# Attention with a relative bias and a bilinear feed-forward: where the third batch's Q and K are transposed, and how the first loads are cut and queued

## The chip, the cores and the metric

The kernel runs on one core of a Trainium2 chip. The metric is the device time of one execution in microseconds (us), as the median of several runs. A profile is taken of one execution; its span runs from the first to the last instruction of the program.

## What is computed

The reference, cut to what matters:

```python
batch, n_heads, seq, head_dim = (8, 8, 576, 64)
scores = scale * np.matmul(q, k.transpose(0, 1, 3, 2))       # scale = 1/8
bucket = np.where(is_small, n, large)                         # n = |i - j|, 32 buckets
scores = scores + bias_table[bucket].transpose(2, 0, 1)[None, :, :, :]
attn = np.exp(scores - np.max(scores, axis=-1, keepdims=True))
attn = attn / (np.sum(attn, axis=-1, keepdims=True) + 1e-09)
x = np.matmul(attn, v)             # to (4608, 512): tokens x (head, dim)
out = (x @ w_a) * (x @ w_b) @ w_out                          # d_ff = 1536
```

All inputs and the output are float32 in HBM; the kernel computes in bfloat16 with float32 sums.

## The kernel before

**Tiling.** Two heads of a batch make a pair: 32 pairs, four to a batch, numbered `p`; pair `p` belongs to batch `p // 4`. The 576 positions of a head are four blocks of 128 ("main") and a tail of 64; the tails of a pair's two heads share one 128-row tile (`ktl`, `qtl`, `vt`) with zeros in the other half. For each pair `qk1` (L330) makes the scores of one block of keys for both heads into one PSUM tile, `ex` (L343) takes the exponential on ScalarE, `mul` (L349) multiplies by the exponential of the bias on VectorE with a reversed window of `W`, `qk_tail`, `ex_tail` and `mul_tail` do the tails, `av` (L385) multiplies by v with a column of ones for the row sum, `norm` (L437) divides, and `t_x` (L452) transposes the result into `xn`. The bias tables `W` and `Wt` come from a small matmul of `bias_table` with a one-hot constant (`oh`, L171 and L216), an exponential (L219), a store to HBM (`bias_tab`) and overlapping reads of it (`load_w`, L165).

**Q and K turned.** The scores need Q and K with the head dimension on partitions. Pairs 0 to 3 are transposed by TensorE in float32 at the start (`q_next`, `k_next`, `tails_next`, L568 to L586). For later batches `early(b)` (L118) decides: where it is true, `t_q` and `t_k` (L282, L302) transpose on TensorE in bfloat16, four blocks each and for `t_k` also the two tail tiles (`t_tails`, L296), and `c_q`, `c_k` copy to `QT` and `KT` on VectorE; where it is false, `turn` (L318) has SyncE's queue transpose a whole batch by DMA into `QTb`, `KTb`, `QTt`, `KTt`. Before, batches 0 and 1 are early; batch 2 is turned by DMA in steps 6 and 7 (`turns`, L692).

**The feed-forward part.** Nine chunks of 512 tokens, each 24 units `ff_a`/`ff_b` (four matmuls into one PSUM bank, read by ScalarE into `ha` or by VectorE into `g_sb`, L505 and L511) and 12 units of `ff_o` (four matmuls each, three units to an output tile, L515). `w_a` and `w_b` lie in `NW` parts of `WC` columns, loaded by `load_w_in` (L156).

**The order of the work** is written out by hand; each engine executes its instructions in the order in which they are recorded. Pairs 0 to 2 run in a loop (L588), pair 3 and the first scores of pair 4 in a listed sequence (L636 to L684), and steps 4 to 32 in a loop (L701) in which step `s` does the scores of pair `s` and the products of pair `s - 1`. A step has markers `U`; at each marker `put_units` emits feed-forward units until the step's quota (6, 7, 7, 7, 6 for steps 4 to 8, then 9) is spread over the step. Unit 24, the first that needs `wo`, falls in step 7.

**Buffers.** PSUM has two tiles for scores, and banks `AV` (one), `TR` (one) and `FF` (two). From step 8 (`ring3`, L707) the feed-forward units use `FF` and `TR` in turn, three banks; then the tail scores of a pair and `av` of blocks 3 and 4 go to `AV` instead of `TR` (L364, L704).

**The loads.** q, k, v and the weights change type while they are loaded, and go by GpSimd's queue, in program order: the tables and v of batch 0, pair 4's q, k and batch 1's tails, two parts of the weights, the rest of batch 1 with the third part between, three parts of weights, batch 2's q and k, `wo`, clears of the second tail tiles, batch 2's tails, and then the later batches. A queue's loads use eight semaphores in turn, so each load issued waits for the one eight before it. The float32 q and k of batch 0 come by SyncE's and ScalarE's queues, the DMA transposes and the output stores by SyncE's.

Of the kernel before, what the change touches and what calls it, by code (L numbers as in the profile page):

```python
# [13 lines left out]
def kernel(  # L14
# [11 lines left out]
    nc = tc.nc  # L26
    FP32 = mybir.dt.float32
    BF16 = mybir.dt.bfloat16
# [78 lines left out]
    KT = [wpool.tile([128, SM + 256], BF16, name=f"KT{i}") for i in range(2)]  # L107
    XG = [wpool.tile([128, 5, 2, Dh], BF16, name=f"XG{i}") for i in range(4)]

    NW = 6  # L110
    WC = DF // NW
    wa_sb = [wpool.tile([128, NMC, WC], BF16, name=f"wa{i}") for i in range(NW)]
    wb_sb = [wpool.tile([128, NMC, WC], BF16, name=f"wb{i}") for i in range(NW)]
# [2 lines left out]
    g_sb = [wpool.tile([128, DM], BF16, name=f"g{df}") for df in range(NDF)]  # L116

    def early(b):  # L118
        return b < 2

    def load_t(src, dst, b, h0, h1):
        for t in range(NM):
            nc.gpsimd.dma_start(  # L123
                out=(vm[b % 2][:, h0:h1, t, 0:Dh] if dst is None else
                     dst[b % 2][:, :].rearrange("p (t h d) -> p t h d", h=H, t=NM)[:, t, h0:h1, :]),
                in_=src[b, h0:h1, 128 * t:128 * t + 128, :].transpose([1, 0, 2]))
# [7 lines left out]
    def load_p(src, dst, b, hp):  # L134
        x = dst[b % 2][:, :].rearrange("p (t h d) -> p t h d", h=H, t=NM)
        for h in (2 * hp, 2 * hp + 1):
            load_h(nc.gpsimd, src, x[:, :, h, :], b, h)

    def load_vp(b, hp):
        for h in (2 * hp, 2 * hp + 1):  # L140
            load_h(nc.gpsimd, v, vm[b % 2][:, h, :, 0:Dh], b, h)

    def load_pad(eng, src, dst, b, nb):
        for hh in range(2):
            eng.dma_start(
                out=dst[64 * hh:64 * hh + 64, 4 * (b % 2):4 * (b % 2) + 4 * nb, hh, 0:Dh],
                in_=src[b:b + nb, hh:H:2, SM:S, :].rearrange("b h c d -> c (b h) d"))

    def load_tails(b, nb):
        load_pad(nc.gpsimd, k, ktl[b // 2 % 2], b, nb)  # L150
        load_pad(nc.gpsimd, q, qtl[b // 2 % 2], b, nb)
# [4 lines left out]
    def load_w_in(part):  # L156
        for src, dst in ((moe_w_a, wa_sb), (moe_w_b, wb_sb)):
            nc.gpsimd.dma_start(
                out=dst[part][:, :, :],
                in_=src[:, WC * part:WC * part + WC].rearrange("(m p) n -> p m n", p=128))  # L160
# [4 lines left out]
    def load_w(eng, hp):  # L165
        eng.dma_start(out=W_sb[hp][:, :, :],
                      in_=bass.AP(tensor=tab, offset=2 * hp * TB, ap=[[1, 128], [TB, 2], [1, 384]]))

    nc.sync.dma_start(out=bt_sb[0:NB, :], in_=bias_table)
    nc.scalar.dma_start(out=cst[:, :], in_=cst_handle.ap())  # L170
    nc.gpsimd.dma_start(out=oh_sb[0:NB, :], in_=oh_handle.ap())  # L171
    def pad(eng, x, n):
        eng.memset(x[0:64, :, 1, 0:n], 0.0)
        eng.memset(x[64:128, :, 0, 0:n], 0.0)
# [17 lines left out]
    pad(nc.vector, qt32, Dh)  # L192
    pad(nc.vector, kt32, Dh)
    load_pad(nc.sync, q, qt32, 0, 1)
    nc.vector.tensor_copy(out=id32[:, :], in_=ident)
    for i in range(2):
        nc.vector.memset(vm[i][:, :, :, Dh:Dh + 1], 1.0)
# [11 lines left out]
    def warm_up(n):  # L209
        for _ in range(n):  # L210
            nc.tensor.matmul(out=warm[:, :], lhsT=zero_sb[:, 0:128], rhs=zero_sb[:, :],
                             start=True, stop=True)

    warm_up(4)
    tps = ps_av.tile([128, 512], FP32, tag="av", name="tab_ps")
    nc.tensor.matmul(out=tps[0:H, 0:NR], lhsT=bt_sb[0:NB, :], rhs=oh_sb[0:NB, :],  # L216
                     start=True, stop=True)
    warm_up(5)
    nc.scalar.activation(out=tab_sb[0:H, 127:127 + NR], in_=tps[0:H, 0:NR], func=ACTF.Exp)  # L219
    nc.scalar.dma_start(out=tab.ap(), in_=tab_sb[0:H, :])  # L220
    load_pad(nc.scalar, k, kt32, 0, 1)

    load_w(nc.gpsimd, 0)
    for hh in range(2):
# [3 lines left out]
    load_vp(0, 0)  # L228
    load_vt(0, 1)
    load_w(nc.gpsimd, 1)  # L230
    load_vp(0, 1)
    load_w(nc.gpsimd, 2)
    load_t(v, None, 0, 4, 8)
    load_w(nc.gpsimd, 3)
    load_p(q, qn, 1, 0)
    load_p(k, kn, 1, 0)
    load_tails(1, 1)
    load_w_in(0)
    load_w_in(1)
    load_vp(1, 0)  # L240
    load_vt(1, 1)
    load_t(q, qn, 1, 2, 8)
    load_t(k, kn, 1, 2, 8)
    load_w_in(2)
    load_t(v, None, 1, 2, 8)

    st = [dict() for _ in range(NP + 1)]
# [27 lines left out]
    def bank(where, dt, name):  # L275
        return where[0].tile([128, 512 if dt is FP32 else 1024], dt, tag=where[1], name=name)
# [5 lines left out]
    def t_q(p, where):  # L282
        if p >= NP or not early(p // 4):
            return
        ps = bank(where, BF16, f"trq{p}")
        for t in range(NM):
            nc.tensor.transpose(ps[:, 128 * t:128 * t + 128], blocks(qn, p)[:, t, :, :], ident)
        st[p]["q"] = ps
# [13 lines left out]
    def t_k(p, where):  # L302
        if p >= NP or not early(p // 4):
            return
        ps = bank(where, BF16, f"trk{p}")
        for t in range(NM):
            nc.tensor.transpose(ps[:, 128 * t:128 * t + 128], blocks(kn, p)[:, t, :, :], ident)
        if p > 3:
            t_tails(p, ps, SM)
        st[p]["k"] = ps  # L310

    def c_k(p, eng=None):
        if p >= NP or not early(p // 4):
            return
        n = SM + 256 if p > 3 else SM
        copy(eng, KT[p % 2][:, 0:n], st[p]["k"][:, 0:n])

    def turn(b, what):  # L318
# [38 lines left out]
    def qk_tail(p):  # L357
        ps = ps_sc.tile([128, 2, 512], FP32, tag="sc", name=f"qkt{p}")
        for t in range(NM):
            nc.tensor.matmul(  # L360
                out=ps[:, 0, :].rearrange("p (h t c) -> p h t c", h=2, t=NM)[:, :, t, :],
                lhsT=kT_(p, t), rhs=qTt_(p), start=True, stop=True)
        nc.tensor.matmul(out=ps[:, 1, :], lhsT=kTt_(p), rhs=qT_(p), start=True, stop=True)  # L363
        pt = bank(TR if p < 8 else AV, FP32, f"qktt{p}")  # L364
        for hh in range(2):
            nc.tensor.matmul(out=pt[:, 0:ST], lhsT=kTt_(p), rhs=qTt_(p)[:, ST * hh:ST * hh + ST],
                             start=(hh == 0), stop=(hh == 1))
        st[p]["ps"] = (ps, pt)
# [252 lines left out]
            t_x(s - 1)  # L621
        qk1(s + 1, 1)

    load_w_in(3)
    load_w_in(4)
    load_w_in(5)
    load_t(q, qn, 2, 0, 8)
    load_t(k, kn, 2, 0, 8)
    load_w_out()
# [6 lines left out]
    ex(3, 0)  # L636
    mul(2, 3)
    mul_tail(2)
    t_q(4, TR)
    c_q(4)  # L640
    t_k(4, FF)
    av(2, 0)
    av(2, 1)
    qk1(3, 2)
    ex(3, 1)
    av(2, 2)
    norm(2, 0)
    c_k(4)
    qk_tail(3)
    ex(3, 2)  # L650
    av(2, 3, FF)
# [6 lines left out]
    t_x(2, FF)  # L658
    mul(3, 1)
    av_part(3, 0)  # L660
    qk1(4, 0)
    av_part(3, 1)
    mul(3, 2)
    av_part(3, 2)
    mul_tail(3)
    ex(4, 0)
    av_part(3, None)
    c_x(2)
    mul(3, 3)
    qk1(4, 1)  # L670
    av_part(3, 3)
# [9 lines left out]
    c_x(3)  # L681
    qk1(4, 3)
    ex(4, 3)
    qk_tail(4)  # L684

    def load_qkt(b):
        load_t(q, qn, b, 0, 8)
# [3 lines left out]

    def turns(s):  # L692
        b = s // 4 + 1
        if b == 2:
            for x in {6: "qk", 7: "t"}.get(s, ""):
                turn(b, x)
        elif 2 < b < B and s % 4 < 3:
            turn(b, "qkt"[s % 4])

    quotas = {4: 6, 5: 7, 6: 7, 7: 7, 8: 6}  # L700
    for s in range(4, NP + 1):  # L701
        new = s < NP
        U = "unit"
        A = lambda *jq: (lambda: [av(s - 1, j, AV if j < 3 or s > 7 else TR) for j in jq])  # L704
        N = lambda j: (lambda: norm(s - 1, j))
        steps = []
        if s == 8:  # L707
            ring3 = True
        if s == 4:
            steps += [U, lambda: ex_tail(4), lambda: mul(4, 0), U, lambda: mul(4, 1), U, lambda: mul(4, 2),  # L710
                      U, lambda: mul(4, 3), lambda: mul_tail(4), U, lambda: t_q(5, TR), lambda: c_q(5),
                      U, lambda: t_k(5, TR), lambda: c_k(5)]
        elif new:
            e = early((s + 1) // 4)
            steps += [lambda: qk(s, 0), lambda: ex(s, 0), U, lambda: ex(s, 1), A(0, 1, 2), N(0), U,
                      lambda: mul(s, 0), A(3, 4), N(3)]
            if s - 1 in XD:
                steps += [lambda: t_x(s - 1), lambda: turns(s)]
            steps += [U, lambda: mul(s, 1), lambda: qk(s, 2), lambda: ex(s, 2)]
            if e:  # L720
                steps += [lambda: t_q(s + 1, TR), lambda: c_q(s + 1)]
            steps += [U, lambda: ex(s, 3)]
            if e:
                steps += [lambda: t_k(s + 1, TR), lambda: c_k(s + 1)]
            steps += [U, lambda: mul(s, 2), U, lambda: mul(s, 3),
                      lambda: qk_tail(s), lambda: ex_tail(s), U]
            if s - 1 not in XD:
                steps += [lambda: t_x(s - 1, TR), lambda: c_x(s - 1), lambda: turns(s)]
            steps += [U, lambda: mul_tail(s), U]
        else:  # L730
            steps += [A(0, 1, 2), N(0), U, A(3, 4), N(3), U, lambda: t_x(s - 1, AV),
                      lambda: c_x(s - 1), U, U, U, U, U, U, U]
        quota = quotas.get(s, 9)
        seen, put = 0, 0
        nu = sum(1 for x in steps if x is U)
        for x in steps:
            if x is U:
                seen += 1
                n = (quota * seen + nu - 1) // nu - put
                put_units(n)  # L740
                put += n
            else:
                x()
        b = s // 4 + 1
        if new and s % 4 == 2 and b + 1 < B:
            load_qkt(b + 1)
        if new and 2 <= b < B:
            if s % 4 == 0:
                load_v(b)
                if b % 2 == 0:  # L750
                    load_vt(b, 2)
# [31 lines left out]
```

## Time and profile before

| | us |
|---|---|
| median of 4 runs (lowest to highest) | 437.63 (436.74 to 438.55) |
| the profiled execution | 438.55 |
| its span | 436.8 |
| TensorE busy | 409.7 (94%) |
| ScalarE / VectorE / GpSimd busy | 241.9 / 192.7 / 122.3 |
| moved by DMA | 43.25 MB, mean 99 GB/s |

The page of the profile gives busy times by engine, then 40 slices of the span with the busy share of each in tenths, then queues, the chain of work that ended last, groups of instructions and DMA issues. PE is TensorE, PEld its weight loads, DVE VectorE, ACT ScalarE, POOL GpSimd, SP SyncE; L12 is line 12 of the kernel. The trace answers closer questions: busy times in given stretches, who waited for whom, instructions in order of time, and DMA packets by queue. Idle time of an engine that is not the bottleneck costs nothing.

### The profile page before, as it was taken

Reading aid. Unit: us, or ns where it says so; the run is one execution under the profiler, and the core shown is the slowest. Engines: PE = TensorE matmul, PEld = TensorE weight load, DVE = VectorE, ACT = ScalarE, POOL = GpSimd, SP = SyncE. Lnnn points to the kernel's source line nnn. Section 1 sums busy time; section 2 is a strip of 40 time slices with the busy share of each in tenths; the row PEclk is TensorE's granted clock in tenths of the full one; section 3 lists DMA queues with packets and bytes.
Section 4 is the critical chain, followed back from the end, with each engine's and each line's share of the span. In section 5 each row is a group of like instructions: output and inputs, shape, how many; then the busy total and the mean of one; then the engine's idle time right before and its main releaser. Section 6 shows DMA issues by size and latency. Waiting matters only on the chain.

```text
span 436.8 us, 8256 instructions
## 1 busy us (share of the span) xinstructions
PE 409.7 (94%) x3271; PEld 201.1 (46%) x3324; DVE 192.7 (44%) x465; ACT 241.9 (55%) x341; POOL 122.3 (28%) x164
## 2 busy tenths in 40 slices
PE   6878997599999999999999999999999999999995
PEld 2555453244444444444444444444444454444442
DVE  3656666034554355425552555355534550430320
ACT  2867566156665666566665666566657642323321
POOL 5897966376204500370027001100000000000000
PEclk9989999689999999999999999999999999999999
DMA  8999999999996991399519930931021001002004
GB/s 166 172 137 133 163 172 160 164 168 141 185 118 46 189 158 39 28 175 148 92 10 155 188 66 15 183 87 39 14 87 40 14 16 76 23 2 96 0 2 96
DMA packets 176711, 43.25 MB, mean 99 GB/s; under 512 B 164104, under 2 KB 171824, under 8 KB 176672
## 3 DMA queue, kind: packets, MB, share of 16 engines
q0 software_dynamic: 111632, 18.72, 60.1%
q1 hardware_dynamic: 63280, 23.56, 30.2%
q10 hardware_dynamic: 1760, 0.43, 0.5%
q8 instruction: 26, 0.43, 0.4%
q14 instruction: 13, 0.11, 0.1%
HBM read 38.80 MB, written 9.45 MB: 110 GB/s over the span
## 4 chain that ended last, share of the span: by engine, by line
PE 85%; DMA 7%; SPq 3%; POOL 2%; issue 1%; DVE 1%; ACT 1%; DVEq 0%; POOLq 0%
PE po L520 21%; PE pa L501 21%; PE pb L501 21%; PE av L405 8%; PE qk L335 7%; PE av L396 3%; DMA KTb<-kn 3%; SPq L327 2%; DMA Wt<-bias_tab 2%; PE qkt L360 1%; PE qkt L363 1%; DMA oh_sb<-oh 1%; DMA qtl<-in_q_dram 1%; POOL vm L123 1%; DMA bias_tab<-tab_sb 1%
## 5 line engine op out<-in xcount | busy, mean ns | idle before, releaser
L346 ACT ACTIVATE at<-qk 128x1024 bf16<-128x1024 f32 x128 | 126.4, 1024 | 31.8 <-PE qk L335 31.8
L513 DVE TENSOR_TENSOR g<-pb,ha 128x512 bf16<-128x512 f32 x108 | 74.7, 691 | 118.3 <-PE pb L501 96.2
L501 PE MATMUL pa<-xn,wa 128*128 128x512 bf16 x420 | 110.5, 380 | 1.1 <-ACT ha L508 0.5
L501 PE MATMUL pb<-xn,wb 128*128 128x512 bf16 x417 | 110.2, 379 | 0.7
L520 PE MATMUL po<-wo,g 128*128 128x512 bf16 x410 | 101.7, 387 | 7.1 <-DMA wo<-in_moe_w_out_dram 5.8
L508 ACT ACTIVATE ha<-pa 128x512 f32<-128x512 f32 x108 | 64.5, 598 | 66.6 <-PE pa L501 66.5
L354 DVE TENSOR_TENSOR at<-at,W 128x512 bf16<-128x512 bf16 (+1 forms) x128 | 60.0, 483 | 11.2 <-ACT at L346 9.6
L520 PEld LDWEIGHTS <-g 128*128 128x128 bf16 x432 | 39.0, 99 | 54.5 <-issue 10.5
L501 PEld LDWEIGHTS <-wa 128*128 128x128 bf16 x432 | 38.9, 98 | 49.4 <-issue 9.2
L524 ACT ACTIVATE ob<-po 128x512 f32<-128x512 f32 x36 | 21.5, 597 | 70.5 <-PE po L520 68.5
L501 PEld LDWEIGHTS <-wb 128*128 128x128 bf16 x432 | 39.0, 98 | 46.0 <-issue 5.9
L123 POOL DMA_DIRECT2D vm<-in_v_dram x32 | 27.4, 879 | 113.5 <-PE av L405 104.6
L405 PE MATMUL av<-vm,at 128*128 128x65 bf16 x992 | 45.0, 195 | 0.0
L405 PEld LDWEIGHTS <-at 128*128 128x128 bf16 x992 | 40.8, 99 | 3.8 <-issue 0.3
L441 DVE RECIPROCAL rc<-av 128x6 f32<-128x6 f32 x64 | 12.0, 188 | 67.1 <-PE av L405 65.3
L396 PE MATMUL av<-vt,att 128*128 128x130 bf16 x156 | 35.3, 227 | 1.1 <-DMA vt<-in_v_dram 0.7
L374 ACT ACTIVATE att<-qkt 128x1024 bf16<-128x1024 f32 x32 | 32.7, 1020 | 0.0
L442 DVE TENSOR_TENSOR XG<-av,rc 128x384 bf16<-128x384 f32 x64 | 31.4, 490 | 2.2
L335 PE MATMUL qk<-QTb,KTb 64*128 64x512 bf16 x192 | 29.4, 385 | 2.5 <-DMA KTb<-kn 2.5
L123 POOL DMA_DIRECT2D kn<-in_k_dram x28 | 24.5, 902 | 9.8 <-DMA vt<-in_v_dram 4.3
L123 POOL DMA_DIRECT2D qn<-in_q_dram x28 | 24.6, 906 | 8.7 <-DMA kn<-in_k_dram 2.8
L396 PEld LDWEIGHTS <-att 128*128 128x128 bf16 x156 | 15.4, 99 | 18.3 <-DVE XG L442 12.7
(103 smaller groups left out, 216.0 us busy)
## 6 DMA issues: line engine op xcount, KB each, us to landing
out_dram<-ob SPq DMA_DIRECT2D x32, 256.0 KB, 3.3
qn<-in_q_dram POOLq DMA_DIRECT2D x24, 128.0 KB, 10.0
kn<-in_k_dram POOLq DMA_DIRECT2D x24, 128.0 KB, 11.8
vm<-in_v_dram POOLq DMA_DIRECT2D x24, 128.0 KB, 6.2
wa<-in_moe_w_a_dram POOLq DMA_DIRECT2D x6, 256.0 KB, 6.7
wb<-in_moe_w_b_dram POOLq DMA_DIRECT2D x6, 256.0 KB, 7.2
wo<-in_moe_w_out_dram POOLq DMA_DIRECT2D x1, 1536.0 KB, 17.6
q<-in_q_dram SPq DMA_DIRECT2D x8, 128.0 KB, 4.1
```

The costliest lines, as they stand in the source:

```text
L123: nc.gpsimd.dma_start(out=(vm[b % 2][:, h0:h1, t, 0:Dh] if dst is None else dst[b % 2][:, :].rearrange("p (t h d) -> p t h d", h=H, t=NM)[ ...
L335: nc.tensor.matmul(out=ps[:, hh, :], lhsT=kT_(p, t)[r, :], rhs=qT[r, :, :], start=True, stop=True)
L346: nc.scalar.activation(out=at[:, :, :], in_=ps[:, :, :], func=ACTF.Exp, scale=scale)
L354: nc.vector.tensor_tensor(out=at[:, :, lo:hi], in0=at[:, :, lo:hi], in1=w[:, :, y:(None if z < 0 else z):-1], op=MULT)
L374: nc.scalar.activation(out=at[:, 0:1024].rearrange("p (a x) -> p a x", a=2), in_=ps[:, :, :], func=ACTF.Exp, scale=scale)
L396: nc.tensor.matmul(out=pav[:, slot, :, :], lhsT=x, rhs=vt[b // 2 % 2][:, 4 * i + hp, :, 0:Dh + 1], start=fresh, stop=True, skip_group_chec ...
L405: nc.tensor.matmul(out=pav[:, slot, hh, :], lhsT=x, rhs=vm[i][:, 2 * hp + hh, t, 0:Dh + 1], start=False, stop=True, skip_group_check=True)
L442: nc.vector.tensor_tensor(out=xg[:, j0:j0 + n, :, :], in0=pav[:, 0:n, :, 0:Dh], in1=rc.unsqueeze(3).to_broadcast([128, n, 2, Dh]), op=MULT)
L501: nc.tensor.matmul(out=ff[key][:, :], lhsT=w[df // FW][:, mc, 128 * (df % FW):128 * (df % FW) + 128], rhs=xn_sb[mc][:, xin(c)], start=(mc ...
L508: nc.scalar.activation(out=ha[:, :], in_=ff["pa"][:, :], func=ACTF.Copy)
L513: nc.vector.tensor_tensor(out=g_sb[df][:, :], in0=ff["pb"][:, :], in1=ff["ha"][:, :], op=MULT)
L520: nc.tensor.matmul(out=po[:, :], lhsT=g_sb[df][:, 128 * tt:128 * tt + 128], rhs=wo_sb[:, df, :], start=(df == 0), stop=(df == NDF - 1))
```

## The change

Batch 2 becomes early too: TensorE transposes its Q and K, pair by pair, and SyncE's four DMA transposes of that batch go. With it the third feed-forward bank starts at step `R3 = 12` instead of 8. The weights lie in three parts of 512 columns. The one-hot is loaded by ScalarE's queue, the k tails of batch 0 by SyncE's instead of ScalarE's, one warm-up matmul is added ahead of the table's, and v of batch 0's later heads comes in four loads instead of six. Pair 4's transposes move from ahead of pair 2's products to after pair 3's last scores, and its tails get a bank and a copy of their own in step 4, where `qk_tail(4)` moves too. The weight loads and the table loads change places as listed.

```diff
-    NW = 6
+    NW = 3
+    R3 = 12
@@ early
-        return b < 2
+        return b < 3
@@ start
-    nc.gpsimd.dma_start(out=oh_sb[0:NB, :], in_=oh_handle.ap())
+    nc.scalar.dma_start(out=oh_sb[0:NB, :], in_=oh_handle.ap())
     load_pad(nc.sync, q, qt32, 0, 1)
+    load_pad(nc.sync, k, kt32, 0, 1)
-    warm_up(4)
+    warm_up(5)
-    load_pad(nc.scalar, k, kt32, 0, 1)
@@ first loads
     load_w(nc.gpsimd, 1)
-    load_vp(0, 1)
+    load_t(v, None, 0, 2, 8)
     load_w(nc.gpsimd, 2)
-    load_t(v, None, 0, 4, 8)
-    load_w(nc.gpsimd, 3)
     load_p(q, qn, 1, 0)
     load_p(k, kn, 1, 0)
+    load_w(nc.gpsimd, 3)
     load_tails(1, 1)
     load_w_in(0)
-    load_w_in(1)
     load_vp(1, 0)
     load_vt(1, 1)
     load_t(q, qn, 1, 2, 8)
     load_t(k, kn, 1, 2, 8)
-    load_w_in(2)
+    load_w_in(1)
     load_t(v, None, 1, 2, 8)
...
-    load_w_in(3)
-    load_w_in(4)
-    load_w_in(5)
+    load_w_in(2)
@@ t_k, c_k: the tails come with the main blocks
-        if p > 3:
+        if p > 4:
@@ qk_tail
-        pt = bank(TR if p < 8 else AV, FP32, f"qktt{p}")
+        pt = bank(TR if p < R3 else AV, FP32, f"qktt{p}")
@@ pair 3
     mul_tail(2)
-    t_q(4, TR)
-    c_q(4)
-    t_k(4, FF)
     av(2, 0)
...
     norm(2, 0)
-    c_k(4)
     qk_tail(3)
...
     av_part(3, 0)
+    c_x(2)
+    t_q(4, FF)
+    c_q(4)
+    t_k(4, FF)
+    c_k(4)
     qk1(4, 0)
+    mul(3, 2)
+    ex(4, 0)
     av_part(3, 1)
-    mul(3, 2)
+    mul_tail(3)
     av_part(3, 2)
-    mul_tail(3)
-    ex(4, 0)
     av_part(3, None)
-    c_x(2)
...
-    qk_tail(4)
+
+    def tails4():
+        ps = bank(TR, BF16, "trt4")
+        t_tails(4, ps, 0)
+        copy(None, KT[0][:, SM:SM + 256], ps[:, 0:256])
@@ turns
-        if b == 2:
-            for x in {6: "qk", 7: "t"}.get(s, ""):
-                turn(b, x)
-        elif 2 < b < B and s % 4 < 3:
+        if 2 < b < B and s % 4 < 3:
@@ steps
-        A = lambda *jq: (lambda: [av(s - 1, j, AV if j < 3 or s > 7 else TR) for j in jq])
+        A = lambda *jq: (lambda: [av(s - 1, j, AV if j < 3 or s >= R3 else TR) for j in jq])
-        if s == 8:
+        if s == R3:
             ring3 = True
         if s == 4:
-            steps += [U, lambda: ex_tail(4), lambda: mul(4, 0), U, lambda: mul(4, 1), U, lambda: mul(4, 2),
+            steps += [U, tails4, lambda: mul(4, 0), U, lambda: qk_tail(4), lambda: ex_tail(4), lambda: mul(4, 1), U, lambda: mul(4, 2),
```

More of the change, by code (lines that the diff above doesn't have):

```diff
@@ L314, in c_k @@
             return
-        n = SM + 256 if p > 3 else SM
+        n = SM + 256 if p > 4 else SM
         copy(eng, KT[p % 2][:, 0:n], st[p]["k"][:, 0:n])
```

## The prediction, made before the result was known

> **What bounds the kernel now.** I read the page first.
>
> ```profile
> PE 409.7 (94%) x3271; PEld 201.1 (46%) x3324; DVE 192.7 (44%) x465; ACT 241.9 (55%) x341; POOL 122.3 (28%) x164
> PE   6878997599999999999999999999999999999995
> PEclk9989999689999999999999999999999999999999
> ```
>
> TensorE is full from the ninth slice on; what can still be won lies in the first 95 us, where PE has gaps and, in slices 7 and 8 (76 to 98 us), a lowered clock. Next the busy times by stretch (us; then PE, PEld, DVE, ACT, POOL, clock, DMA):
>
> ```profile
> 57.98:67.95 9.97, 9.86 (x99) 5.24 (x100) 6.12 (x15) 7.19 (x10) 7.79 (x14) 1.00 2.16 160
> 67.95:74.20 6.25, 6.20 (x69) 3.12 (x69) 3.75 (x10) 3.94 (x7) 4.57 (x6) 1.00 1.49 179
> 74.20:80.10 5.90, 0.07 (x2) 0.01 (x1) 1.49 (x3) 1.02 (x2) 0.00 (x0) 0.83 1.19 155
> 80.10:88.20 8.10, 5.63 (x21) 2.26 (x23) 0.39 (x2) 1.74 (x3) 4.28 (x6) 0.71 1.73 156
> 88.20:93.80 5.60, 5.53 (x56) 2.95 (x57) 1.08 (x3) 1.94 (x2) 3.85 (x5) 0.70 1.78 180
> 148.98:194.00 45.02, 44.63 (x380) 21.55 (x386) 21.51 (x52) 28.61 (x42) 11.34 (x14) 1.00 1.09 104
> ```
>
> The first row is pair 6's step, the last is four later steps; PE is full in both. The hole is 74.2 to 93.8. The waits of PE there, and then those before 48 us:
>
> ```profile
> PE po L520 <- DMA wo<-in_moe_w_out_dram: 5.8, 1, 5.8
> PE qk L335 <- DMA KTb<-kn: 2.5, 1, 2.5
> ...
> PE tab_ps L216 <- DMA oh_sb<-oh: 2.0, 1, 2.0
> PE trk L307 <- DMA kn<-in_k_dram: 1.2, 1, 1.2
> PE trq L287 <- DMA qn<-in_q_dram: 0.9, 1, 0.9
> ```
>
> PE wants `wo` at 74.2 and gets it at 80.0, then wants batch 2's turned K at 85.7 and gets it at 88.2. The chain of waits from 60 to 95 us shows where that K came from, and GpSimd's timeline where the loads were issued:
>
> ```profile
> 65.62 9.73 SPq L327
> 75.53 12.58 DMA KTb<-kn
> 88.16 0.95 PE qk L335 x4
> ```
> ```profile
> 62.46 1.03 POOL L163 DMA_DIRECT2D wo<-in_moe_w_out_dram  x1
> 67.15 1.38 POOL L145 DMA_DIRECT2D ktl<-in_k_dram  x2
> 68.49 1.39 POOL L145 DMA_DIRECT2D qtl<-in_q_dram  x2
> ```
>
> The DMA view gives `wo` 17.6 us to landing (80.0) and the tails `ktl`, `qtl` of batch 2 medians of 14.5 and 15.6 (81.3 to 85.1). They are slow because two queues share the engines; the DMA view of 71 to 74 us, q0 GpSimd's queue, q1 the transposes (packets, MB, share):
>
> ```profile
> q0 software_dynamic: 451, 0.46, 107.9%
> q1 hardware_dynamic: 447, 0.11, 45.5%
> ```
>
> Packet for packet. So this stage is bound by GpSimd's load queue, slowed by the DMA transposes; after 94 us PE's work alone sets the end.
>
> **What the Trainium skill says.** "DMA: Bandwidth & Descriptors", section "Queues, rings and completion order": each engine serves its queue rows in turn, packet by packet. The 451 to 447 packets agree. The same page, "Issuing engine by pattern": loads from ScalarE's or SyncE's queue are generally faster than GpSimd's. Agrees: the 32 KB one-hot took 3.8 us from GpSimd, the 32 KB `cst` 1.8 from ScalarE. "TensorE: Matmul & The Clock Gate", Part 1: an idle window of about 3.4 us halves the clock, a busy one restores it. Agrees in kind: after 5.8 idle us the four `po` matmuls took 1.89 us instead of 1.03. The same page, Part 4: a 128x128 transpose takes about 275 ns in a kernel. The trace differs for a row of them: each lasts 219 ns but four start within 0.23 us, 56 ns each, and I use that.
>
> **The change part by part**, against the profiled 438.55 us (span 436.8, 1.75 outside it), which stands 0.9 above the median of 437.63.
>
> *Start.* The one-hot leaves ScalarE's queue at 1.2 and lands at 3.0 (1.8 as `cst`). Five warm-ups (four took 1.89 from 1.2, less an overlap of the last: 0.43 each) end at 3.4, so the table matmul starts at 3.4 instead of 5.05: 1.65 earlier, and table, exponentials and first `W` load with it. Queued behind the one-hot on ScalarE are pair 0's two k loads: 0.55 later, landing at 6.6, when the next five warm-ups end (6.5): nothing. The k tails leave ScalarE (1.4 us of issue, idle there) for SyncE ahead of eight loads of pairs 2 and 3; these landed from 9.9 and are used from 16.2, so the cover is 4 us. If gone: at most 1.4.
>
> *Pair 4's transposes* (L287, L307) move behind pair 3's last scores, its tails into a bank of their own with one more DVE copy (0.38, under FFN matmuls). PE's waits 0.9 + 1.2 + 0.2 go, and with them ScalarE's 3.9 before its third exponential of pair 3. PE then reaches the FFN about 4 us earlier (1.65 + 2.3). Bounds: 1.65, or 6 if ScalarE's whole idle time counts.
>
> *Larger loads.* Weights: 12 issues become 6; v of batch 0: 6 become 4; one-hot moved. At 0.75 us per issue GpSimd saves 6.7 us, but only the 1.5 of v lie before the first weight load; from 30 us on the queue is behind (latencies grow from 4.8 to 10), and saved issue time is hidden. Rows double from 512 to 1024 B: at 52 to 57 us 512 B rows already move 197 GB/s, and `wo`'s 1024 B rows beside transposes 198 in sum; I take no gain (bounds: 0, or 10% of the 16 us that weights take). Wider parts arrive later for their first user, in return: 0.5 MB more at 197 GB/s is 2.7 us before `pb`; with the stream earlier and PE earlier this evens out, and any wait here comes out of the one below.
>
> *Batch 2 on PE.* Gone: the transposes QTb, KTb and the two tails' (SyncE 19 us), and the 2.5 us wait. Added: 10 transposes per pair, 0.55 us of PE, four times; two DVE copies (0.41 + 0.55), DVE being 53% busy. The new wait: `t_k(8)` in step 7, just ahead of the first `po`, needs `ktl` and `qtl`, and these are queued behind `wo` on GpSimd. Behind it on PE stand `po`, pair 7's tail scores and pair 8's scores, so ScalarE and VectorE run dry as well. Without the cover of anything else this wait is the new limit. When does it end?
> The last q, k load of batch 2 landed at 69.7 (61.6 + 8.1). The stream starts 1.65 to 3.15 earlier; I take 2.5: 67.2. `wo`, 1.5 MB at 197 GB/s: 8.0; pair 6's output transposes, which stood behind KTb on SyncE, now fall into it: 640 packets at 1.5 ns (447 of them cost 3.0 us less 451 x 5.2 ns): 1.0. The tails: 2048 rows of 128 B; at 61 to 66 us the queue did 5986 in 5 us: 1.7. Sum 78.0 (from 73 to 82, as the stream's lead may be 6 or none and gaps come in).
> PE is there at 74.2 - 4 + 0.55 = 70.8, so it idles some 7 us and starts cold.
> From there to the mark 93.8 PE has 20 `po` matmuls (0.216 each, 4.3), qk 0.54, tail scores 0.49, five av blocks of 0.30: 6.9 us at full clock. Before, 80.1 to 93.8 took 13.7: 2.5 waiting and 4.3 cold. After: one cold stretch of about 5 us, 2.5 lost (1.7 to 3.4). 78.0 + 6.9 + 2.5 = 87.4, 6.4 earlier. Pairs 9 to 11 then pay 3 x 0.55 = 1.65.
>
> *Two FFN banks for pairs 8 to 11* (three before, for 33 units). Pairs 5 to 7 ran with two and 7 units each: 9.97 us, against 45.02 / 4 - 2 x 0.865 = 9.53 for the same work turned by DMA; the 0.44 is already less than the 0.55 of transposes, so two banks cost nothing there. With 9 units three stand back to back once per pair; I take 0.25 per pair, 0.75 in all (0 to 10).
>
> Sum: 6.4 - 1.65 - 0.75 = 4.0. 438.55 - 4.0 = 434.5 profiled, 433.6 against the median.
>
> **The rivals.**
> *No stall.* The loads are there when PE is (70.8). Then 70.8 + 6.9 = 77.7, 16.1 earlier, less 2.4: 423.9. For it: both stalls are DMA waits and a competitor leaves. Against: the queue would have to be 7 us faster, and 52 to 57 us shows it at its full rate without competitor. Halfway (tails at 74, a short stall) gives 429.
> *Wait for wait.* The tails come at 82: 82 + 6.9 + 2.5 = 91.4, 2.4 earlier, all spent: 437.6. For it: GpSimd paused at 36 to 38 us for earlier loads to land, and with larger pieces such pauses can grow. Against: the transposes that slowed `wo` are gone.
> *Slower, by the banks.* In steps 8 to 11 a unit may start only when the bank of the one before last is read, by ScalarE (0.60, behind exponentials of 1.02) or VectorE (0.69). If each of 33 units waits 0.3, that is 9.9: 4.75 - 9.9, so 442.8. It decides from 0.14 per unit. Against: pairs 5 to 7.
>
> **How the numbers follow.** A measurement tells about 0.3% (1.3 us) from none. Forecast (430 to 436.3) 0.58; no stall or halfway 0.20; wait for wait (436.3 to 439) 0.11; banks 0.11. Faster 0.78, same 0.11, slower 0.11. The range leaves out the full no-stall case and the banks at full price: 427.5 to 438.5.
>
> **What would show it.** The table matmul at 3.4; no PE wait for `qn`, `kn` of pair 4; no `QTb` transfer before 80 us; one PE wait at the tail transposes of pair 8 for `qtl` or `ktl`, ending near 78, and a clock near 0.5 after it; steps 9 to 11 of about 11.8 us each. The forecast is wrong if that wait ends before 74 or after 82, or if PE waits for FFN banks after it.

## The result and the profile after

| | before | after |
|---|---|---|
| median beside each other (lowest to highest) | 438.31 (435.82 to 441.05) | 436.77 (434.13 to 439.68) |
| ratio, 95% interval | | 0.9963 (0.9952 to 0.9974) |
| profiled execution, its span | 438.55, 436.8 | 437.56, 435.8 |

The change gains 1.6 us (438.31 x 0.0037), not 4.0. First the page of the kernel after:

```profile
PE 411.3 (94%) x3311; PEld 202.7 (47%) x3365; DVE 196.6 (45%) x474; ACT 241.8 (55%) x341; POOL 116.2 (27%) x155
PE   8796899499999999999999999999999999999995
PEclk9998999699999999999999999999999999999999
```

The hole is still in the eighth slice (76 to 87 us): PE has a 4 there, where before there were a 7 and a 5 in the seventh and eighth, and the clock in it is 0.6. A second, smaller one has come into the fourth slice: a 6 where before there was an 8. The waits of PE in the kernel after (total, times, longest, us):

```profile
PE trk L298 <- DMA ktl<-in_k_dram: 5.9, 1, 5.9
PE pa L500 <- DMA xn<-XG: 2.6, 1, 2.6
PE av L395 <- DMA vt<-in_v_dram: 1.7, 1, 1.7
...
PE trk L298 <- DMA qtl<-in_q_dram: 0.3, 1, 0.3
```

As forecast, the two waits (`wo` and the turned K) have become one, for batch 2's tails at the transposes of pair 8, and pair 4's `qn` and `kn` are no longer waited for. New is a wait of 2.6 for pair 1's output `xn` in the first feed-forward unit. The busy times by stretch (us; PE, PEld, DVE, ACT, POOL, clock, DMA):

```profile
67.61:75.00 7.39, 7.34 (x78) 3.79 (x78) 4.40 (x13) 5.09 (x8) 6.24 (x9) 1.00 1.39 185
75.00:82.40 7.40, 1.25 (x9) 0.57 (x7) 1.05 (x2) 1.50 (x2) 1.95 (x3) 0.80 1.97 164
82.40:91.37 8.97, 8.88 (x77) 4.69 (x79) 2.84 (x8) 3.57 (x5) 7.31 (x9) 0.79 1.98 143
140.31:185.32 45.01, 44.62 (x379) 21.55 (x384) 21.49 (x52) 28.61 (x41) 11.90 (x15) 1.00 1.14 105
```

PE is full to 76.0, stands until 82.4 but for one transpose, and needs 8.97 us to the mark (pair 8's scores, 91.37; before 93.82) for work of about 6.9 by the prediction's count. It resumes at a lowered clock: the granted clock was 0.50 from 82.4 to 86.0, and the first four `po` matmuls took 1.91 us, four later ones 1.04. Four later steps take 45.01, as before (45.02). GpSimd's timeline in the kernel after shows what the tails stood behind:

```profile
58.46 0.88 POOL L124 DMA_DIRECT2D kn<-in_k_dram  x1 [0.73 <-DMA wa<-in_moe_w_a_dram]
61.68 0.88 POOL L124 DMA_DIRECT2D kn<-in_k_dram  x1 [2.35 <-DMA wb<-in_moe_w_b_dram]
63.85 1.02 POOL L164 DMA_DIRECT2D wo<-in_moe_w_out_dram  x1 [1.29 <-DMA qn<-in_q_dram]
...
68.53 1.37 POOL L146 DMA_DIRECT2D ktl<-in_k_dram  x2
```

The landings, from the trace: batch 2's last k load 71.64 (before 69.69, forecast 67.2), `wo` 79.49, the tails 82.34 (before 85.07, forecast 78.0).

### The profile page after: what moved, and what is told of

Read it like the earlier page. It is cut to its first block, busy times and chain, and to the rows that moved or that the text cites. A ratio compares the mean times of both kernels' runs of the same rounds, so it can differ in the third digit from the quotient of the medians.

```text
span 435.8 us, 8337 instructions
## 1 busy us (share of the span) xinstructions
PE 411.3 (94%) x3311; PEld 202.7 (47%) x3365; DVE 196.6 (45%) x474; ACT 241.8 (55%) x341; POOL 116.2 (27%) x155
## 4 chain that ended last, share of the span: by engine, by line
PE 79%; DMA 13%; POOL 5%; issue 1%; ACTq 0%; DVE 0%; ACT 0%
PE po L519 22%; PE pa L500 19%; PE pb L500 19%; PE av L404 7%; PE qk L334 6%; DMA qn<-in_q_dram 3%; DMA qtl<-in_q_dram 3%; PE av L395 3%; DMA wb<-in_moe_w_b_dram 3%; DMA wa<-in_moe_w_a_dram 2%; DMA vm<-in_v_dram 2%; PE qkt L359 1%; PE qkt L362 1%; DMA k<-in_k_dram 1%; DMA bias_tab<-tab_sb 1%
## 5 line engine op out<-in xcount | busy, mean ns | idle before, releaser
L519 PE MATMUL po<-wo,g 128*128 128x512 bf16 x410 | 100.5, 383 | 1.2
L404 PE MATMUL av<-vm,at 128*128 128x65 bf16 x992 | 43.8, 193 | 0.0
L404 PEld LDWEIGHTS <-at 128*128 128x128 bf16 x992 | 39.7, 97 | 4.1
L334 PE MATMUL qk<-QTb,KTb 64*128 64x512 bf16 x160 | 24.2, 381 | 0.0
L395 PEld LDWEIGHTS <-att 128*128 128x128 bf16 x156 | 15.2, 98 | 17.6 <-DVE XG L441 10.7
```

Source lines behind the costliest of these rows:

```text
L334: nc.tensor.matmul(out=ps[:, hh, :], lhsT=kT_(p, t)[r, :], rhs=qT[r, :, :], start=True, stop=True)
L395: nc.tensor.matmul(out=pav[:, slot, :, :], lhsT=x, rhs=vt[b // 2 % 2][:, 4 * i + hp, :, 0:Dh + 1], start=fresh, stop=True, skip_group_chec ...
L404: nc.tensor.matmul(out=pav[:, slot, hh, :], lhsT=x, rhs=vm[i][:, 2 * hp + hh, t, 0:Dh + 1], start=False, stop=True, skip_group_check=True)
L519: nc.tensor.matmul(out=po[:, :], lhsT=g_sb[df][:, 128 * tt:128 * tt + 128], rhs=wo_sb[:, df, :], start=(df == 0), stop=(df == NDF - 1))
```

## The experiments

All ran in rounds against the kernel before, whose median was 438.0 to 438.4 in every set. Theory 1 is the prediction's: the landing of batch 2's tails on GpSimd's queue sets the end. Theory 2: the larger weight parts slow the queue. Theory 3: the earlier start is real, and lost in the middle of the stream.

**Is it the start, the size of the parts, the amount of loads, or the banks?** Four edits of the changed kernel; the landings are those of each one's profiled execution.

```diff
@@ e1_store: the table is stored from GpSimd's queue
-    nc.scalar.dma_start(out=tab.ap(), in_=tab_sb[0:H, :])
+    nc.gpsimd.dma_start(out=tab.ap(), in_=tab_sb[0:H, :])
@@ e2_six_parts: six parts, two for each of the three loads, in the same places
-    NW = 3
+    NW = 6
@@ e3_less_weight: the third part of w_a and w_b is not loaded, the second is used again
-    load_w_in(2)
+            nc.tensor.matmul(out=ff[key][:, :], lhsT=w[min(df // FW, 1)][:, mc, ...
@@ e4_r16: two feed-forward banks for four pairs more
-    R3 = 12
+    R3 = 16
```

> The changed kernel with the bias table stored to HBM from GpSimd's queue instead of ScalarE's, so that the store need not wait for a q load of pair 0 (it was issued at 6.14 us, 1.3 us after the exponential before it). Theory 1 (the load queue's lead was lost ahead of 31 us, half of it by this wait): the first W load goes out at about 8.0 instead of 9.7, the tails of pair 8 land 1 to 2 us earlier (80.5 to 81.5 instead of 82.3), the time falls by as much: 435 to 436. Theory 2 (the larger weight parts made the queue late): no change in the tails' landing beyond 0.5 us, 436.8. Theory 3 (the queue is full from 30 us on, so a lead at its start is absorbed): the same, 436.8.

> The changed kernel with the input weights in six parts as before, loaded in the same places (parts 0 and 1 where the first third went, and so on). Theory 1: rows of 512 B move as fast as rows of 1024 B, so the tails of pair 8 land within 1 us of 82.3 and the time stays at 436.8 within 1 us. Theory 2: smaller rows let the transposes of pair 1's output through twice as fast beside them (they took 10.2 us, 3.7 before) and GpSimd does not pause 2.95 us at 36 us; the tails land 2 us earlier or more, and the time is about 434.5.

> The changed kernel without the last third of the input weights' loads: the last four of the twelve column blocks use the middle third again, so the feed-forward result is another one, and 1 MB less passes the queue ahead of the tails of pair 8. Theory 1: the tails land 5.2 us earlier (1 MB at 197 GB/s), near 77, PE waits 0.7 us or less for them (it is there at 76.0), stays at full clock, and the time falls by the wait of 6.2 and the cold clock's 2: about 429. Theory that something else in that stage is just behind (wo, exponentials, pair 8's copies): less than 5 us gained.

> The changed kernel with the third feed-forward bank from step 16 instead of 12: four more steps of nine units with two banks, and without any transposes. The record's estimate of 0.25 us per pair: 1.0 us slower, 437.8. If two banks cost nothing (as steps 9 to 11 of the changed kernel suggest, 0.5 us longer each with 0.55 of transposes in them): 436.8. The slower rival, 0.3 us per unit: 10.8 us slower, 447.

| | us | ratio (interval) | batch 1's tails land | last k of batch 2 | batch 2's tails |
|---|---|---|---|---|---|
| after | 436.77 | 0.9963 (0.9952 to 0.9974) | 31.76 | 71.64 | 82.34 |
| e1_store | 436.96 | 0.9969 (0.9953 to 0.9986) | 29.14 | 69.88 | 81.43 |
| e2_six_parts | 436.32 | 0.9967 (0.9949 to 0.9985) | 28.55 | 70.01 | 82.11 |
| e3_less_weight | 427.70 | 0.9779 (0.9753 to 0.9804) | 28.64 | 62.82 | 73.45 |
| e4_r16 | 436.17 | 0.9951 (0.9932 to 0.9970) | 27.85 | 69.46 | 80.40 |
| before | 438.12 | | 30.27 | 69.69 | 85.07 |

e3 leaves out a third of the input weights' loads and so computes another result, with as many matmuls. With 1 MB less in the queue its tails land 9 us earlier and the time falls by 9. Expected were 5.2 and about 8; of the 8.9 us by which the tails came earlier, 3.1 are there at batch 1's tails already, ahead of what is left out, since the changed kernel's own profiled execution was late there. PE's wait there is all but gone:

```profile
PE trk L298 <- DMA qtl<-in_q_dram: 0.9, 1, 0.9
```

So the queue's end does set the time (theory 1). e2 is no different from the change, so theory 2 falls as the explanation of the lost gain. Pair 1's output transposes, which took 3.7 us before and 10.2 in the changed kernel, still take 8.7 in e2, beside weight rows of 512 bytes: not the larger rows alone make them slow. From step 12's tail exponential to step 16's e4 took 45.04 with two banks, the kernel before 45.02 with three: banks cost nothing here. And e1, e2 and e4 all begin with a lead of 1.1 to 2.4 us at batch 1's tails and have none at the last k load: theory 3. The changed kernel's own profiled execution had no lead even at batch 1's tails (31.76, before 30.27), so one execution's landing can be off by 2 us or more.

**Each half alone.** e5_pe_part is the kernel before with batch 2 turned by TensorE and the later bank switch that goes with it; e6_rest the changed kernel with batch 2 turned by DMA and the switch at step 8.

```diff
@@ e5_pe_part, against before
-        return b < 2
+        return b < 3
-        if b == 2:
-            for x in {6: "qk", 7: "t"}.get(s, ""):
-                turn(b, x)
-        elif 2 < b < B and s % 4 < 3:
+        if 2 < b < B and s % 4 < 3:
...
-        if s == 8:
+        if s == 12:
...
@@ e6_rest, against after: the same lines the other way, and R3 = 8
```

> The kernel before with only batch 2 turned by TensorE (and its later bank switch); one-hot, k tails, loads, weight parts and pair 4 as before. Theory 1 (the landing of batch 2's tails sets the end, nothing else is lost): the last k load still lands at 69.7 and wo near 79, and with the turned K and Q gone the tails land near 81.5 instead of 85.1; PE waits from 74.2 to there, reaches the mark qk1(8,2) at 90.5 instead of 93.8, and loses 1.0 in steps 8 to 11: 435.8, that is 0.995 of before, as much as the whole change or more. Theory 3 (the other parts hold a real lead, lost somewhere in the middle) gives the same here but expects the rest of the change by itself to gain 1 or 2. A rival: the tails land where they did, at 85, and the time is 438 to 439.

> The changed kernel with batch 2 turned by the DMA again (bank switch at step 8): what the one-hot, the three weight parts, the fewer loads and pair 4's move give without the PE part. The prediction's lead of 2.5 us, if it were there, would move the turned K from 88.2 to 85.7 and give 435.6. If the lead is absorbed before batch 2's q and k are in (theory 3), the last k load lands at 70 to 71.6, the turned K at 88 to 90, and the time is 437.5 to 439.5: no gain, or a loss of 1.

e5: 437.69, 1.0002 (0.9983 to 1.0021); last k 69.60, tails 81.27. e6: 437.47, 0.9984 (0.9968 to 1.0000); last k 70.00, the turned K 87.38 (before 88.11). The landings came near those expected by theories 1 and 3 (e6's turned K just ahead of its 88 to 90); neither half gains anything that can be told from none. e5 missed its 435.8 by 1.9: it reached the mark at 91.36, not 90.5, and lost 1.8 from there to step 12, not 1.0. The waits of PE in e5:

```profile
PE trk L299 <- DMA ktl<-in_k_dram: 6.1, 2, 5.8
```

**Another order.** e8_tails_first puts the tails ahead of `wo` and the first use of `wo` into step 8.

```diff
     load_t(k, kn, 2, 0, 8)
-    load_w_out()
...
     load_tails(2, 2)
+    load_w_out()
-    quotas = {4: 6, 5: 7, 6: 7, 7: 7, 8: 6}
+    quotas = {4: 6, 5: 6, 6: 6, 7: 6, 8: 6}
```

> The changed kernel with the tails of batch 2 issued ahead of wo, and one FFN unit fewer in each of steps 5, 6 and 7, so that the first use of wo lies in step 8 behind pair 8's first scores. Nothing is saved on the queue; only its order and PE's order change. Theory 1: the tails land 8 us earlier, near 74.3; PE arrives there near 73.5 and waits 1; wo lands near 82.3, and PE wants it near 80: together 3 us of waiting instead of 6.2, and less time at a low clock: near 433. A rival, that the wait for the tails only becomes one for wo: PE stands until 82.3 all the same, and the time is 436 to 437.

437.33, 0.9972 (0.9956 to 0.9989). The rival was right: the tails land at 72.95, and PE waits for `wo`, which lands at 83.60, as long as it had for them:

```profile
PE po L519 <- DMA wo<-in_moe_w_out_dram: 6.2, 1, 6.2
```

**Who takes the lead?** Something in the middle must. SyncE's queue transposes the attention outputs of pairs 0, 1 and 4 to 7, 640 packets each, beside the loads; pairs 2 and 3 are turned by TensorE in both kernels. e7_output_by_pe lets TensorE turn all of them.

```diff
-    XD = {0, 1, 4, 5, 6, 7} | set(range(8, NP - 1))
+    XD = set(range(8, NP - 1))
@@ pairs 0 to 2
-            t_x(s - 1)
+            t_x(s - 1, FF)
+            c_x(s - 1)
```

> The changed kernel with the attention outputs of pairs 0, 1 and 4 to 7 turned by TensorE (as pairs 2 and 3 are) instead of by DMA: pairs 0, 1, 4, 5, 6 put 5 x 640 transposed packets among the packets of GpSimd's queue ahead of batch 2's tails. At 1.5 ns a packet that is 4.8 us: if the queue is busy all the while, the tails land near 77.5 instead of 82.3, PE's wait of 6.2 shrinks to 1 or 2, and PE's added transposes (5 per pair, 0.3 each, partly in idle time) take 1.5 back: near 433.5. If what absorbs the lead is not the queue's packets but the pauses of GpSimd, which issues a load only when the one eight before it has landed, the tails move by 2 or less, and the time is 436 to 437.

429.33, 0.9806 (0.9781 to 0.9830): last k 64.61, tails 74.17, no wait for tails at all, mean clock 0.999. More than expected (433.5): the transposes cost more than the 4.8 that I gave them. The next runs divide it up: in `XD` only some pairs are taken out, in the changed kernel and in the one before.

```diff
@@ e9_output_pe_01, against after (with the edit of pairs 0 to 2)
+    XD = {4, 5, 6, 7} | set(range(8, NP - 1))
@@ e10_output_pe_456, against after
+    XD = {0, 1, 7} | set(range(8, NP - 1))
@@ e11_before_output_pe: e7's edit on the kernel before
@@ e12_output_pe_not7, against after (with the edit of pairs 0 to 2)
+    XD = set(range(7, NP - 1))
@@ e13_before_pe_01: e9's edit on the kernel before
@@ e14_pe_part_output_pe: e7's edit on e5
@@ e15_output_pe_0145, against after (with the edit of pairs 0 to 2)
+    XD = set(range(6, NP - 1))
```

> The changed kernel with the outputs of pairs 0 and 1 alone turned by TensorE; pairs 4 to 7 by DMA. All six of them on TensorE made the last k load land at 64.6 and the tails at 74.2. Theory (each transposed packet in the queue's way costs about 1.5 ns, wherever it falls while the queue is busy): 1280 packets fewer bring k and tails 1.9 earlier, to about 68 and 80; the time falls by 1.5 to 435. A rival, that these two pairs do special harm because in the changed kernel they run into the first large weight part (10.2 us each instead of 3.7): 4 us or more, time 433 or less.

> The changed kernel with the outputs of pairs 4, 5 and 6 alone turned by TensorE. By the price of 1.5 ns a packet: 1280 packets fewer ahead of the last k load (2 us, it lands at 68), 640 more ahead of wo and the tails (tails 2.9 earlier, 79); the time falls by 2, less 0.5 for TensorE's work: 435. By the rival of the run before (pairs 0 and 1 do the harm) it falls by 1 or less.

> The kernel before with the outputs of pairs 0, 1 and 4 to 7 turned by TensorE, as in the run that gave 429.3 on the changed kernel. wo lands at about 75 instead of 80.0, where PE wants it near 75: that wait goes. The turned K, which needs the last k load (near 65) and two DMA transposes behind it in the full queue, lands at 80 to 82 instead of 88.2 and is wanted near 80. Time 431 to 432.5: then the change is worth 2 to 3 us once the load queue no longer sets the end. If the change's parts save nothing even then: 429 to 430, the same as the changed kernel so treated. If the turned K still lands past 86: 436.

> The changed kernel with the outputs of pairs 0, 1, 4, 5 and 6 turned by TensorE, pair 7's by DMA again, since by then the tails are in: five transposes and two copies less in step 8 (0.3 of PE), and 640 packets among loads that nothing waits for. 429.0, or the same as with pair 7 too; more than 430 if a load or a turn behind it is late after all.

> The kernel before with the outputs of pairs 0 and 1 alone turned by TensorE. Theory: these transposes cost the queue nothing in the kernel before (the loads around them landed no earlier without them: 57.8 and 57.9 for a weight part, 60.8 and 61.2 for another), and about 2.5 us in the changed kernel, which is where its lead goes. Then the last k load stays at 69 to 70 and the time within 0.3% of before, 437.5 to 438.5. If they cost 1.5 ns a packet here as well, k lands at 67.8 and the time is 436 to 436.5.

> The kernel before with batch 2 turned by TensorE and the outputs of pairs 0, 1 and 4 to 7 too; one-hot, loads, weight parts and pair 4 as before. The changed kernel so treated took 429.3, the kernel before 436.6. Theory: without output transposes the start's lead of 2 to 2.8 us at the last k load is real, so this kernel, which lacks it, has k at 67.4, wo near 75, tails near 77, waits for them 2 to 3 us, and takes 431 to 432. If the start's parts are worth nothing even so, it takes 429 to 430.

> The changed kernel with the outputs of pairs 0, 1, 4 and 5 turned by TensorE, pairs 6 and 7 by DMA. Pair 6's transposes fall on wo and the tails. By the prediction's term they cost 1.0: k near 65, tails 10.7 later near 76, PE waits 1 or less, 430. If they cost what one run showed (15.2 from k to tails instead of 9.7 without them), the tails land near 80 and the time is 433 to 434.

| | us | ratio (interval) | last k | tails |
|---|---|---|---|---|
| e9: after, 0, 1 | 433.71 | 0.9862 (0.9815 to 0.9909) | 66.98 | 82.15 |
| e10: after, 4 to 6 | 430.12 | 0.9809 (0.9771 to 0.9847) | 66.94 | 76.63 |
| e12: after, 0, 1, 4 to 6 | 429.41 | 0.9779 (0.9749 to 0.9810) | 65.88 | 75.60 |
| e15: after, 0, 1, 4, 5 | 428.48 | 0.9788 (0.9756 to 0.9820) | 64.47 | 73.98 |
| e11: before, all six | 436.63 | 0.9954 (0.9933 to 0.9974) | 67.38 | 82.23 |
| e13: before, 0, 1 | 437.31 | 0.9983 (0.9961 to 1.0004) | 68.33 | 83.16 |
| e14: before and batch 2 on PE, all six | 432.40 | 0.9875 (0.9838 to 0.9911) | 67.94 | 77.66 |

e9's profiled execution, 437.23, is the slowest of its six (from 430.26), so its landings are the late end of that kernel, and no cost below is worked out from them. e13 fell between its two theories: its last k load, 1.4 earlier than before, is nearer the 67.8 of the price per packet than the 69 to 70 of no cost. Most of that lead, 1.2, is there at batch 1's tails (29.12 against 30.27), so, as far as single executions tell, these transposes cost the kernel before next to nothing from 30 us on. e10 gains more than expected, e11 less: its turned K lands at 85.40, not at 80 to 82, since it queues behind another transpose and beside `wo`. In e14 PE waits 3.9 in all:

```profile
PE trk L299 <- DMA ktl<-in_k_dram: 3.0, 1, 3.0
...
PE trk L299 <- DMA qtl<-in_q_dram: 0.9, 1, 0.9
```

What two pairs' transposes do is seen from 28 to 36 us, in the queues of the kernel after and of e15 (packets, MB, share):

```profile
q0 software_dynamic: 1973, 1.09, 124.6%
q1 hardware_dynamic: 573, 0.13, 21.4%
```
```profile
q0 software_dynamic: 3655, 1.37, 147.4%
```

With 573 transposed packets in the way GpSimd's queue moved 0.28 MB less: an estimate of 1.4 us at the 0.197 MB per us that it did alone from 52 to 57 us in the kernel before, 2.5 ns a packet. e7 and e12, also without them, moved 1.43 and 1.29. The same stretch in the kernel before and in e13:

```profile
q0 software_dynamic: 2898, 1.12, 120.4%
q1 hardware_dynamic: 640, 0.15, 10.6%
```
```profile
q0 software_dynamic: 2985, 1.15, 124.1%
```

There it moves as little without transposes: 1.12 MB in 8 us are 140 GB/s, so in this stretch the stream is not at its limit, and they cost it nothing. All these runs but e3, which loads less, and e9, e10 and e13, which treat only some of the four pairs, give the landing of the last k load:

| | outputs 0, 1, 4, 5 by DMA | by TensorE | their cost |
|---|---|---|---|
| start as before | 69.69, 69.60 (e5) | 67.38 (e11), 67.94 (e14): 67.7 | 2.0 |
| start as changed | 69.46 to 71.64, mean of six (after, e1, e2, e4, e6, e8) 70.2 | 64.47, 64.61, 65.88: 65.0 | 5.2 |
| lead of the change | -0.5 | 2.7 | |

Each is the landing of one execution, and the six spread over 2.2 us. So theory 3 holds, and what takes the lead is named: it is 2.7 us where these transposes are gone, and the same four pairs' output transposes, which cost 2.0 in the kernel before, cost 5.2 in the changed one. The times agree: by the medians, taking all six off the queue gives 1.8 on the kernel before (e11) and 7.4 on the changed one (e7). And the rest of the change is worth something then: from e14 to e7, with the same outputs on TensorE, 3.1 us over two sets, where with the outputs on the DMA it was 0.9 (e5's 437.69 to 436.77). From e14 to e15, in one set, it is 3.9, but e15 also leaves pairs 6 and 7 to the DMA.

The lowest median is e15's, though e7 and e12 can't be told from it. Its page, where the clock stays at 9 and PE's row has nothing under 8 after the second slice:

```profile
PE   8688999999999999999999999999999999999995
PEclk9999999999999999999999999999999999999999
```

## Why the prediction was wrong, step by step

*What bounds the kernel* was right. Profiled times follow the landing of batch 2's tails: 77.66 gave 433.9 (e14), 80.40 gave 435.3 (e4), 82.34 gave 437.56 (after); e10 with 76.63 gave 430.2, having the changed start as well. Forecast for a landing at 78.0 was 434.5.

*The start* failed in part. The table matmul began at 3.44 (forecast 3.4), but the first `W` load was issued at 9.73, not 7.75 (before 9.40). In all kernels with the changed start it left at 8.65 to 9.73, with the table's store issued anywhere from 5.1 to 6.2 (6.5 before): from the store to that load it takes 2.7 to 3.9 us, 4.2 in e1. On ScalarE's queue the store was issued at 6.14, 1.3 after its exponential: its semaphore, one of eight that ScalarE's and SyncE's queues take in turn, had last been used by pair 0's first k load, the last part of which landed at 6.03. That load had gone behind the one-hot, for which the prediction counted nothing. But e1 shows that another queue for the store changes nothing. What lead there is at batch 1's tails, about 1.0 without transposes (28.1 against 29.0 in the runs of the last table and of e7), is nearer the v loads saved (1.5) than the first `W` load (0.2 earlier in the same runs); the two were not tried apart.

*The lead of the stream* is the step that failed: "The stream starts 1.65 to 3.15 earlier; I take 2.5: 67.2". The last k load landed at 71.64 in the profiled run, 70.2 in the mean of six: a lead of none in place of 2.5. So the tails' wait ended at 82.4, past the 82 that the prediction had set as its own limit. The prediction carried a lead at the start unchanged through 60 us of a shared resource. It counted pair 6's transposes, which it saw changing place, and not those of pairs 0, 1, 4 and 5, which were in both kernels; but the changed stream lost its lead to them. Why they cost it more is argued from the stretch at 28 to 36 us: there they fell on a queue that moved more without them, and before on one with slack. One price for all packets did not hold either: 1.5 ns, from one stretch, against 5.2 us for 2560 packets, 2.0 ns, in the changed kernel and 0.8 in the one before. That the lead without them, 2.7, is close to the 2.5 taken is in part luck: 1.0 of it came from the start.

*From the last k load to the tails* it forecast 10.8 and got 10.7 (`wo` 7.85 and tails 2.85 for 8.0, 1.0 and 1.7). Without pair 6's transposes in it, it is 9.5 to 9.7 (e7, e10, e12, e14, e15); the other kernels that keep them, turn batch 2 by TensorE and leave the order as it is have 10.6 to 12.1 (e1 to e5), and e9's late execution 15.2. The term of 1.0 was 1.1 in the profiled run and 1.0 to 2.5 elsewhere. In e15 pair 6's transposes are issued at 72.5, when the tails are nearly in, and cost nothing.

*From the tails to the mark* 9.4 was forecast, 8.97 came.

*The costs of the PE part and the banks*: 2.4 forecast, 1.8 measured. From the mark to step 12's tail exponential it took 47.14 before and 48.94 after. That is the 1.65 forecast for the transposes of pairs 9 to 11 and nearly nothing for the banks, which cost nothing in e4 either, though in other steps. The rival by the banks is out.

*Pair 4's move* took its waits away, but PE did not come 4 us earlier. It waited 1.7 for `vt` near 20 us, began its first feed-forward unit 2.4 earlier than before (35.52, before 37.95), and then waited 2.6 for `xn` of pair 1, whose transpose took 10.2 us (3.7 before). It began pair 5's scores 1.3 later than before (49.36 against 48.08) and reached the tails' transposes at 76.0, not 70.8. These waits ended ahead of the hole and cost nothing while the tails set the end. In e10, where they nearly don't, 2.2 of the wait for `xn` is left; in e12 and e15 it is gone.

The sum in the profiled run: tails 4.3 later than forecast, 0.4 from the shorter way to the mark and 0.6 from transposes and banks: 4.0 - 4.3 + 0.4 + 0.6 = 0.7. At step 12's tail exponential the profiled runs differ by 0.65 (140.96 and 140.31), in all by 1.0. The rival "wait for wait" (tails at 82, 437.6) describes what came, with another cause than the pauses that it named: e7's GpSimd pauses for weight parts about as long as the changed kernel's (9.5 us in all and 3.0 at the longest, 10.1 and 3.0 there), and its last k load lands 5.6 before the mean of the six all the same.

What stays open: why the lead grows from 1.0 at 28 us to 2.7 at 65 when nothing is in its way, and whether the earlier start or the larger weight parts make the transposes cost more. From 28 to 36 us the streams with parts of 512 columns and without transposes moved 1.29 to 1.43 MB, those with 256 columns 1.06 to 1.15 with or without them, e2 among them (1.14). So the larger parts, for which the prediction took no gain, may be where the lead grows; e2 without the transposes would tell, and was not run. How pairs 0 and 1 and pairs 4 and 5 share the 5.2 is open too: e10, without those of pairs 4 to 6, has its last k load 3.3 ahead of the mean of six. That the place of each transpose decides its cost was not tried by shifting a transpose by itself.

## What to carry to other kernels

Where a load queue sets the end, list everything that shares its DMA engines up to that moment, the unchanged traffic too, before a lead at the start is carried to the end: traffic that cost little before can take the whole lead of the changed stream. Changes to one queue can be worth little alone and much together: by the medians batch 2 on TensorE gave 0.5 us and the rest of the change 0.8, neither to be told from none, the outputs on TensorE 1.8, all three 9. And moving the awaited load ahead in a full queue only changes the name of the wait (e8).

## What the runs showed of the hardware

- Transposes by DMA can hold up the loads of another queue by more than their bytes say. The Trainium skill, "DMA: Bandwidth & Descriptors", section "Queues, rings and completion order", has each engine serve its queues in turn, packet by packet; the 451 and 447 packets that the prediction shows side by side agree. The runs show what that can cost: 2.0 to 2.5 ns for each of the transposed packets, most of them of 256 bytes, in the changed kernel. By their bytes alone it would be 1.3 ns, an estimate at the 197 GB/s that the load queue moved alone. In the kernel before it was 0.8 ns.
- The transposes are held up as well: pair 1's took 10.2 us beside the first weight part in the changed kernel, 8.7 beside rows half as long (e2), and 3.7 in the kernel before.
- A store of 8 KB and the start of the load that waits for it were 2.5 to 3.9 us apart beside the first loads, 4.2 with the store on GpSimd's queue.
- Two PSUM banks for nine feed-forward units a step were as good as three (45.04 and 45.02 us for four steps).
